# D added to the raw filter, its transposes evacuated in halves, and a new sequence, in a four-layer long-convolution and MLP kernel

## The chip, the cores and the metric

The kernel runs on one core of a Trainium2 chip. Its engines are TensorE (PE in the profile, PEld its weight loads), VectorE (DVE), ScalarE (ACT), GpSimd (POOL) and SyncE (SP), which here only issues DMAs. The metric is the device time of one execution in microseconds (us). The time before is the median of three runs, 240.48 us (239.6, 240.48 and 241.68).

## The reference

The input x is 2048 positions by 512 channels in bfloat16, and four layers are applied to it, each added to its input: A, B, A, B.

```python
def _A_ref(q, k, v, shift_k, ssm_k, ssm_D):
    for t in range(ks):                       # ks = 4
        k_shift = k_shift + k_pad[:, t:t + S, :] * shift_k[:, ks - 1 - t]
    kv = k_shift * v
    y = irfft(rfft(pad(kv)) * rfft(pad(ssm_k)))[:S]     # causal convolution, 2048 taps per channel
    y = y + kv * ssm_D
    return q * y

def _B_ref(x, w1, b1, w2, b2):                # 512 -> 1376 -> 512
    h = gelu(einsum(layernorm(x), w1) + b1)
    return einsum(h, w2) + b2

x = x + A(layernorm(x), k, v, ...);  x = x + B(layernorm(x), ...)
x = x + A(layernorm(x), k, v, ...);  x = x + B(layernorm(x), ...)
```

Only q of layer A depends on x; the convolution y depends on k, v and the filter alone, so it is the same for both A layers.

## The kernel before, in words

The kernel computes y once, in front, and then walks through the 16 groups of positions (a group is 128 positions, one per partition) twice: normalise, multiply by y and add (layer A), normalise and run the MLP (layer B).

**The convolution** is a length-4096 Fourier transform made of matmuls. The filter (ssm_k, 512 channels by 2048) arrives in four slabs b = 0..3 of 128 channels, 512 KB each, in the region R_HRAW. For each slab 16 transposes (tag "ht", line 523), each on every sixteenth column, turn it into two PSUM banks; one copy (BOTH, that is ACT or DVE, line 450) moves it to R_HP; an add (line 447) of D on one partition row then puts the skip term kv * D into the filter's tap 0. Stage 1 (h1, line 540) takes 16 matmuls per eight channel groups into a two-bank tile, 16 tiles in all, each emptied by one "evac" (line 450); stage 2 (h2, line 553) is 16 tiles of eight matmuls with weights from tab_s, 16 slabs of 256 KB. Sixteen DMAs from SBUF to SBUF then make a half-swapped copy of the filter's spectrum.

The shifted k times v is made in two ways: for channel blocks 0 and 1 by transposes (line 584), matmuls with tap diagonals (line 601) and a DVE multiply out of PSUM (line 608), for blocks 2 and 3 by eight DVE operations each on 128 x 2048 elements (line 447). Its stage 1 (x1, line 540 again) and stage 2 (x2, line 646) follow; after stage 2 come 16 DVE products with the filter's spectrum (line 447, called "the products"), which read four rotating buffers; then the inverse stages i1 (line 669) and i2 (line 726).

**The layers.** Per group of positions: bn_stats and bn_aggr on DVE (749, 751), a power on POOL (755, 757), a normalising tensor_scalar (763), the products with y (447); then z is transposed by PE (809) or by DMA (802), m1 (822) with its Gelu on ACT (827) and m2 (855) with its add on DVE (859).

**Warm-up.** Before the filter lands, PE multiplies a tile of zeros eight times (line 496); POOL clears the tile (line 490).

**The order of the work.** Every operation is recorded by P.op with the regions it reads and writes. A written-out table, ORDER, gives the sequence of all operations; each engine executes its own in that sequence, in order. SECOND names the operations that go to the second of their two allowed engines, and BANKS the first PSUM bank of every tile. Waits are derived from these: an operation that reuses a bank waits for the reader of the tile that had it last. SP also issues its DMAs in this order, so a DMA that waits holds back the ones behind it.

The change and the prediction touch the filter's transposes and the D add (516 to 530), the zero tile (489, 490), the table preload (462), the DMA queues, and the order of everything up to about 85 us. The region R_T2 of the inverse table (L444) overlies k.

Of the kernel before, what the change touches and what calls it, by code (L numbers as in the profile page):

```python
# [7 lines left out]
ALU = mybir.AluOpType  # L8
# [30 lines left out]
class Prog:  # L39
# [280 lines left out]
def _tables():  # L320
# [32 lines left out]
    T2 = np.stack([np.cos(ps), -np.sin(ps)], 2) / 2048  # L353
    T2 = T2.reshape(128, 4096)
    return F, S2, U, T2


AR = 105600
PE_CH, PO_CH = (0, 1), ()
LOADS = ("k", "v") + tuple(range(16))  # L360
PARTS = ((0, 64), (64, 64))
BLOCKS0, BLOCKS1 = (1,1,2,2,2,2,2,2,2), (4, 4, 4, 4)
NSPLIT = 4


def bass_interleave_layers__ssm_conv_h3__mixer_channel_mlp__prompt_kernel(
        nc, A_q, A_k, A_v, A_shift_k, A_ssm_k, A_ssm_D, B_x, B_w1, B_b1, B_w2, B_b2, out):
    P = Prog(nc)
# [54 lines left out]
    R_W = place(512)  # L423
# [29 lines left out]
    BOTH = (ACT, DVE)  # L453
# [442 lines left out]
```

## Time and profile before

| | us |
|---|---|
| median of three runs | 240.48 |
| the profiled execution | 239.94 |
| its span | 238.1 |
| PE busy | 226.6 |
| DVE busy | 177.2 |
| ACT busy | 141.8 |
| POOL busy | 32.5 |

The span runs from the first to the last instruction of the program; the profiled execution's own time has 1.84 us around it. A line such as "4.99 1.86 PE L523 ... x16" says: from 4.99 us on, for 1.86 us, sixteen instructions of line 523 on PE; in brackets stands how long the engine was idle before and what ended the wait. Lines of a helper (447 for element-wise operations, 450 for evictions, 436 and 444 for DMAs) gather many steps; the operand shapes tell them apart.

### The profile page before, as it was taken

Reading aid. Unit: us, or ns where it says so; the run is one execution under the profiler, and the core shown is the slowest. Engines: PE = TensorE matmul, PEld = TensorE weight load, DVE = VectorE, ACT = ScalarE, POOL = GpSimd, SP = SyncE. Lnnn points to the kernel's source line nnn. Section 1 sums busy time; section 2 is a strip of 40 time slices with the busy share of each in tenths; the row PEclk is TensorE's granted clock in tenths of the full one; section 3 lists DMA queues with packets and bytes.
Section 4 is the critical chain, followed back from the end, with each engine's and each line's share of the span. In section 5 each row is a group of like instructions: output and inputs, shape, how many; then the busy total and the mean of one; then the engine's idle time right before and its main releaser. Section 6 shows DMA issues by size and latency. Waiting matters only on the chain.

```text
span 238.1 us, 5549 instructions
## 1 busy us (share of the span) xinstructions
PE 226.6 (95%) x2312; PEld 152.1 (64%) x2332; DVE 177.2 (74%) x360; ACT 141.8 (60%) x225; POOL 32.5 (14%) x70
## 2 busy tenths in 40 slices
PE   7997999977999999999999999999999999999996
PEld 3886777866899886867577676554444444444544
DVE  0799999999999999999987799959271783311124
ACT  2599999999999983746246552474335245067000
POOL 1140000001013431332120130040022001000000
PEclk9999999999999999999999999999999999999999
DMA  6999947999990005120222022205104003301033
GB/s 222 367 347 383 384 120 201 293 283 270 379 310 2 3 3 67 21 51 0 44 44 47 0 48 44 45 1 69 22 0 88 3 0 65 111 0 47 6 110 105
DMA packets 37035, 27.40 MB, mean 115 GB/s; under 512 B 19506, under 2 KB 29969, under 8 KB 37010
## 3 DMA queue, kind: packets, MB, share of 16 engines
q1 hardware_dynamic: 36446, 26.91, 38.7%
q8 instruction: 18, 0.29, 0.5%
q10 hardware_dynamic: 564, 0.14, 0.4%
q14 instruction: 7, 0.06, 0.1%
HBM read 16.82 MB, written 2.10 MB: 79 GB/s over the span
## 4 chain that ended last, share of the span: by engine, by line
PE 81%; ACT 13%; DMA 2%; DVE 2%; issue 2%
PE ps L822 32%; PE ps L855 31%; ACT ar L450 12%; PE ps L669 5%; PE ps L540 4%; PE ps L726 3%; PE ps L601 2%; DMA ar<-in_A_ssm_k_dram 2%; PE ps L523 1%; PE ps L844 1%; DVE ar L450 1%; PE ps L646 1%; PE ps L553 1%; ACT L462 1%; DVE ar L608 1%
## 5 line engine op out<-in xcount | busy, mean ns | idle before, releaser
L827 ACT ACTIVATE ar<-ps,sm 128x256 bf16<-128x256 f32 (+4 forms) x143 | 66.1, 524 | 70.2 <-PE ps L822 66.4
L822 PE MATMUL ps<-ar 128*128 128x256 bf16 (+3 forms) x567 | 82.1, 296 | 0.2
L855 PE MATMUL ps<-ar 128*128 128x512 bf16 (+1 forms) x330 | 78.2, 379 | 0.7
L450 ACT ACTIVATE ar<-ps 128x1024 bf16<-128x1024 f32 (+2 forms) x80 | 73.2, 1065 | 5.3 <-PE ps L508 3.6
L822 PEld LDWEIGHTS ps<-ar 128*128 128x128 bf16 (+1 forms) x572 | 53.0, 100 | 28.9 <-ACT ar L827 1.2
L447 DVE TENSOR_TENSOR ar<-ar 128x512 bf16<-128x512 bf16 (+3 forms) x106 | 64.9, 640 | 1.0
L855 PEld LDWEIGHTS ps<-ar 128*128 128x128 bf16 (+1 forms) x341 | 33.2, 98 | 35.1
L859 DVE TENSOR_TENSOR ar<-ar,ps 128x512 bf16<-128x512 bf16 x31 | 20.8, 678 | 37.5 <-PE ps L855 37.5
L749 DVE BATCH_NORM_STATS2 sm<-ar 128x6 f32<-128x512 bf16 (+1 forms) x68 | 43.1, 649 | 0.6
L763 DVE TENSOR_SCALAR ar<-ar,sm 128x512 bf16<-128x512 bf16 x64 | 24.7, 403 | 8.3 <-POOL sm L757 6.7
L757 POOL TENSOR_TENSOR sm<-sm 128x2 f32<-128x2 f32 (+2 forms) x26 | 20.6, 790 | 2.2
L755 POOL TENSOR_SCALAR sm<-sm 128x2 f32<-128x2 f32 (+2 forms) x26 | 5.4, 209 | 111.5 <-DVE sm L751 111.1
L540 PE MATMUL ps<-ar 128*64 128x128 bf16 x512 | 16.8, 220 | 0.4 <-ACT ar L450 0.2
L540 PEld LDWEIGHTS ps<-ar 128*64 128x64 bf16 x512 | 14.8, 110 | 2.2 <-ACT ar L450 0.4
L669 PE MATMUL ps<-ar 128*128 128x128 bf16 x256 | 15.1, 220 | 0.9 <-ACT ar L450 0.9
L669 PEld LDWEIGHTS ps<-ar 128*128 128x128 bf16 x256 | 14.6, 114 | 1.3 <-ACT ar L450 0.8
L450 DVE CAST ar<-ps 128x1024 bf16<-128x1024 f32 (+1 forms) x13 | 14.9, 1175 | 0.0
L450 DVE COPY ar<-ps 128x2048 bf16<-128x2048 bf16 (+1 forms) x7 | 7.0, 995 | 7.2 <-PE ps L523 6.9
L646 PE MATMUL ps<-ar 128*128 128x64 bf16 x256 | 9.3, 193 | 2.6 <-ACT ar L450 2.6
L751 DVE BATCH_NORM_AGGREGATE sm<-sm 128x2 f32<-128x6 f32 (+1 forms) x64 | 10.6, 174 | 1.0
L646 PEld LDWEIGHTS ps<-ar 128*128 128x128 bf16 x256 | 8.1, 98 | 3.7 <-ACT ar L450 3.5
L553 PE MATMUL ps<-ar 128*128 128x128 bf16 x128 | 8.6, 219 | 0.2
(33 smaller groups left out, 73.7 us busy)
## 6 DMA issues: line engine op xcount, KB each, us to landing
ar<-tab_s SPq DMA_DIRECT2D x16, 256.0 KB, 10.1
ar<-ar SPq DMA_DIRECT2D x16, 256.0 KB, 4.8
ar<-in_A_ssm_k_dram SPq DMA_DIRECT2D x4, 512.0 KB, 5.9
ar<-in_A_k_dram SPq DMA_DIRECT2D x8, 256.0 KB, 7.5
ar<-in_A_v_dram SPq DMA_DIRECT2D x8, 256.0 KB, 10.1
ar<-in_A_q_dram SPq DMA_DIRECT2D x4, 512.0 KB, 7.1
out_dram<-ar SPq DMA_DIRECT2D x7, 256.0 KB, 2.0
ar<-in_B_w_dram SPq DMA_DIRECT2D x1, 1376.0 KB, 8.8
```

What stands on the lines that cost most here:

```text
L447: return P.op(eng, lambda e: e.tensor_tensor(o, a, b, op), reads=[a, b] + list(more), writes=[o])
L450: f = {ACT: lambda e: e.activation(dst, src(), AF.Copy), DVE: lambda e: e.tensor_copy(dst, src())}
L540: r = e.matmul(Q(tl, 64 * ri, 64, i * 128, [1, 128]), w, m, start=True, stop=True)
L646: r = e.matmul(Q(tl, 0, 128, i * pitch, [1, n]), w, m, start=True, stop=True)
L669: r = e.matmul(Q(tl, 0, 128, i * 128, [1, 128]), w, m, start=q == 0, stop=q == 1)
L749: P.op(DVE, lambda e, sj=sj, x=x: e.bn_stats(sj, x), reads=[x], writes=[sj])
L757: P.op(POOL, lambda e: e.tensor_tensor(r, v, hf, ALU.pow), reads=[v, hf], writes=[r])
L763: P.op(DVE, lambda e: e.tensor_scalar(o, x, m, r, ALU.subtract, ALU.mult), reads=[x, m, r], writes=[o])
L822: r = e.matmul(Q(tl, 0, rows, 0, [1, w]), a, m, start=dk == 0, stop=dk == 3)
L827: P.op(ACT, lambda e, dst=dst, tl=tl, rows=rows, bias=bias, w=w: e.activation(dst, Q(tl, 0, rows, 0, [1, w]), AF.Gelu_apprx_tanh, bias=bia ...
L855: r = e.matmul(Q(tl, 0, 128, 0, [1, 512]), ins[fc][0], ins[fc][1], start=fc == 0, stop=fc == 10)
L859: P.op(DVE, lambda e, x=x, tl=tl: e.tensor_tensor(x, x, Q(tl, 0, 128, 0, [1, 512]), ALU.add), reads=[x], writes=[x], tile=tl)
```

## The change

It does four things.

1. **D.** The four D adds on one partition row of R_HP are gone. In their place four matmuls with one column each turn D into a column per slab (tile "dcol"), and four DVE adds on 128 x 1 elements put them into column 0 of the raw slabs, ahead of the transposes that read that column.
2. **Halves.** Each slab's 16 transposes are two groups of eight (columns 15 to 8, then 7 to 0), each with one bank and its own copy. Only the second group reads the column with D.
3. **Zero tile.** It is 128 x 128 and may be cleared by DVE or POOL; the warm-up matmuls read it four times over as a 128 x 512 operand. The number and size of the warm-up matmuls is as before.
4. **ORDER, SECOND and BANKS** are new. The sequence is another one up to the first m1 tiles and the same behind them, but for the numbers.

```diff
+HSPLIT = (0, 1, 2, 3)
-    z = A(0, 128, R_W, [1, 512])
-    P.op(POOL, lambda e, z=z: e.memset(z, 0.0), writes=[z])
+    z = A(0, 128, R_W, [1, 128])
+    z4 = A(0, 128, R_W, [0, 4], [1, 128])
+    P.op((DVE, POOL), lambda e, z=z: e.memset(z, 0.0), writes=[z])
...
-            r = e.matmul(Q(tl, 0, 128, 0, [1, 512]), z[:, :128], z, start=True, stop=True)
+            r = e.matmul(Q(tl, 0, 128, 0, [128, 4], [1, 128]), z, z4, start=True, stop=True)
...
+    P.tag = "dcol"
+    dcol = Tile(1)
+    ins = [A(0, 1, R_D + 128 * b, [1, 128]) for b in range(4)]
+
+    def f(e, ins=ins):
+        for b in range(4):
+            r = e.matmul(Q(dcol, 0, 128, b, [1, 1]), ins[b], one[:, :1], start=True, stop=True)
+        return r
+    P.op(PE, f, reads=[one] + ins, tile=dcol).preds[warm.i] = "psum"
+    for b in range(4):
+        h = A(0, 128, R_HRAW + b * 2048, [1, 1])
+        P.op(DVE, lambda e, h=h, b=b: e.tensor_tensor(h, h, Q(dcol, 0, 128, b, [1, 1]), ALU.add),
+             reads=[h], writes=[h], tile=dcol)
...
     for b in range(4):
-        tl = Tile(2)
-        src = [A(0, 128, R_HRAW + b * 2048 + a, [16, 128]) for a in range(16)]
...
-        o = A(0, 1, R_HP + b * 2048, [64, 32], [1, 4])
-        tt(o, o, A(0, 1, R_D + 128 * b, [4, 32], [1, 4]), ALU.add, (DVE, POOL))
+        cuts = ((15, 14, 13, 12, 11, 10, 9, 8), (7, 6, 5, 4, 3, 2, 1, 0)) if b in HSPLIT else (tuple(range(15, -1, -1)),)
+        for cut in cuts:
+            tl = Tile(len(cut) // 8)
+            a0 = cut[-1]
+            src = [(a, A(0, 128, R_HRAW + b * 2048 + a, [16, 128])) for a in cut]
+
+            def f(e, src=src, tl=tl, a0=a0):
+                for a, x in src:
+                    r = e.transpose(QB(tl, 0, 128, (a - a0) * 128, [1, 128]), x, IDN)
+                return r
+            P.op(PE, f, reads=[x for _, x in src] + [IDN], tile=tl).preds[warm.i] = "psum"
+            evac(BOTH, A(0, 128, R_HP + b * 2048 + 4 * a0, [4, len(cut)], [64, 32], [1, 4]),
+                 lambda tl=tl, n=len(cut): QB(tl, 0, 128, 0, [128, n], [4, 32], [1, 4]), tl)
```

Line numbers move: in the changed kernel the warm-up is line 499, dcol 511, its adds 516, the taps 524 (508 before), the filter's transposes 542 (523 before), h1 and x1 557 (540), evictions 452 (450), element-wise operations 449 (447), DMAs 438 and 446 (436 and 444), i1 686 (669).

**The opening, PE and DVE.** PE before, from the warm-up to the end of h1:

```order
L496 MATMUL ps<-ar 128x512 x8
L523 MATMUL ps<-ar 128x128 x16
L508 MATMUL ps<-ar 128x512 x2
L523 MATMUL ps<-ar 128x128 x16
L540 MATMUL ps<-ar 64x128 x64
L523 MATMUL ps<-ar 128x128 x32
L540 MATMUL ps<-ar 64x128 x192
```

and PE now:

```order
L499 MATMUL ps<-ar 128x512 x8
L511 MATMUL ps<-ar 128x1 x4
L542 MATMUL ps<-ar 128x128 x8
L524 MATMUL ps<-ar 128x512 x2
L542 MATMUL ps<-ar 128x128 x24
L557 MATMUL ps<-ar 64x128 x48
L542 MATMUL ps<-ar 128x128 x8
L557 MATMUL ps<-ar 64x128 x32
L542 MATMUL ps<-ar 128x128 x24
L557 MATMUL ps<-ar 64x128 x176
```

The dcol matmuls stand ahead of all transposes, the first slab's second half comes behind the taps, and three of the last slabs' halves stand between two h1 groups. DVE, before, up to its first shift products (128x2048):

```order
L450 COPY ar<-ps 128x16x32x4
L447 TENSOR_TENSOR ar<-ar 1x32x4
L450 COPY ar<-ps 128x16x32x4
L447 TENSOR_TENSOR ar<-ar 128x512
L450 CAST ar<-ps 128x128x8
L450 COPY ar<-ps 128x16x32x4 x2
L450 CAST ar<-ps 128x128x8 x3
L447 TENSOR_TENSOR ar<-ar 128x2048 x5
```

and DVE now:

```order
L493 MEMSET ar 128x64
L516 TENSOR_TENSOR ar<-ar,ps 128x1
L452 COPY ar<-ps 128x8x32x4
L516 TENSOR_TENSOR ar<-ar,ps 128x1
L452 COPY ar<-ps 128x8x32x4 x2
L452 CAST ar<-ps 128x128x8
L516 TENSOR_TENSOR ar<-ar,ps 128x1 x2
L452 COPY ar<-ps 128x8x32x4 x4
L452 CAST ar<-ps 128x128x8 x3
L449 TENSOR_TENSOR ar<-ar 128x2048 x5
```

Seven of the eight half copies are on DVE, the tap diagonal (128x512) has gone to POOL, and the h1 evictions (128x128x8) on DVE are four as before. The 128x8x32x4 CAST that followed later on DVE (one h2 tile) is gone; that tile is on ACT now.

**ACT's start.** Before, from its DMA issues to the second stage of the filter (128x8x32x4):

```order
L444 DMA ar<-tab_small 128x384
L436 DMA ar<-in_A_shift_k_dram 1x2048
L436 DMA ar<-in_A_ssm_D_dram 1x512
L436 DMA ar<-in_A_shift_k_dram 128x2x4
L450 ACT_TABLE_LOAD
L450 ACTIVATE ar<-ps 128x512 x2
L450 ACTIVATE ar<-ps 128x128x8 x2
L462 ACT_TABLE_LOAD
L450 ACTIVATE ar<-ps 128x128x8 x10
L450 ACTIVATE ar<-ps 128x16x128
L450 ACTIVATE ar<-ps 128x8x32x4 x13
```

and now (line 464 is the preload, 462 before):

```order
L446 DMA ar<-tab_small 128x384
L438 DMA ar<-in_A_ssm_D_dram 1x512
L438 DMA ar<-in_A_shift_k_dram 1x2048
L464 ACT_TABLE_LOAD
L438 DMA ar<-in_A_shift_k_dram 128x2x4
L452 ACTIVATE ar<-ps 128x512 x2
L452 ACTIVATE ar<-ps 128x8x32x4
L452 ACTIVATE ar<-ps 128x128x8 x12
L452 ACTIVATE ar<-ps 128x16x128
L452 ACTIVATE ar<-ps 128x8x32x4 x15
```

One table load is left, ahead of all evictions; one half copy (the first 128x8x32x4) has come to ACT.

**SP, from the last loads of v to the half-swaps (64x8x256).** Before:

```order
L436 DMA ar<-in_A_v_dram 128x1024 x3
L444 DMA ar<-tab_s 128x1024 x4
L436 DMA ar<-in_B_b_dram 128x10x1
L436 DMA ar<-ar 64x8x256 x8
L444 DMA ar<-tab_small 128x1024
L436 DMA ar<-ar 64x8x256 x3
```

and now:

```order
L438 DMA ar<-in_A_v_dram 128x1024 x2
L446 DMA ar<-tab_s 128x1024
L446 DMA ar<-tab_small 128x1024
L446 DMA ar<-tab_s 128x1024
L438 DMA ar<-ar 64x8x256
L438 DMA ar<-in_B_b_dram 128x10x1
L438 DMA ar<-ar 64x8x256 x6
```

The first quarter of the inverse table (tab_small, 128x1024) stands ahead of the last slab of tab_s; it waits for DVE's last read of k in the shifts.

More of the change, by code (lines that the diff above doesn't have):

```diff
@@ L45 @@
     ORDER = (
[41 rows of a table removed]
[42 rows of a table added]
     SECOND = (
-        53, 56, 57, 59, 62, 63, 65, 66, 78, 84, 88, 98, 112, 162, 172, 174, 186, 188, 208, 240, 276, 317, 342, 385)
+        61, 63, 67, 69, 71, 73, 75, 81, 87, 89, 93, 171, 179, 181, 197, 209, 223, 249, 281, 316, 351, 394)
     BANKS = (
[7 rows of a table removed]
[7 rows of a table added]
     def __init__(self, nc):
@@ L487, in bass_interleave_layers__ssm_conv_h3__mixer_channel_mlp__prompt_kernel, with f @@
     tload(t_sm, row, 384, R_U, 256)
-    z = A(0, 128, R_W, [1, 512])
-    P.op(POOL, lambda e, z=z: e.memset(z, 0.0), writes=[z])
+    z = A(0, 128, R_W, [1, 128])
+    z4 = A(0, 128, R_W, [0, 4], [1, 128])
+    P.op((DVE, POOL), lambda e, z=z: e.memset(z, 0.0), writes=[z])
     P.tag = "warm"
     tl = Tile(2)
-    def f(e, tl=tl, z=z):
+    def f(e, tl=tl, z=z, z4=z4):
         for i in range(8):
-            r = e.matmul(Q(tl, 0, 128, 0, [1, 512]), z[:, :128], z, start=True, stop=True)
+            r = e.matmul(Q(tl, 0, 128, 0, [128, 4], [1, 128]), z, z4, start=True, stop=True)
         return r
@@ L500, in bass_interleave_layers__ssm_conv_h3__mixer_channel_mlp__prompt_kernel @@
     one = A(0, 1, R_ONE, [1, 128])
-    P.op(POOL, lambda e: e.memset(one, 1.0), writes=[one])
+    P.op((POOL, DVE), lambda e: e.memset(one, 1.0), writes=[one])
+    P.tag = "dcol"
[10 more added lines that the diff above has]
+             reads=[h], writes=[h], tile=dcol)
     P.tag = "taps"
@@ L517, in bass_interleave_layers__ssm_conv_h3__mixer_channel_mlp__prompt_kernel @@
     for b in range(4):
-        tl = Tile(2)
-        src = [A(0, 128, R_HRAW + b * 2048 + a, [16, 128]) for a in range(16)]
-        def f(e, src=src, tl=tl):
-            for a in range(16):
-                r = e.transpose(QB(tl, 0, 128, a * 128, [1, 128]), src[a], IDN)
-            return r
-        P.op(PE, f, reads=src + [IDN], tile=tl).preds[warm.i] = "psum"
-        evac(BOTH, A(0, 128, R_HP + b * 2048, [4, 16], [64, 32], [1, 4]),
-             lambda tl=tl: QB(tl, 0, 128, 0, [128, 16], [4, 32], [1, 4]), tl)
-        o = A(0, 1, R_HP + b * 2048, [64, 32], [1, 4])
-        tt(o, o, A(0, 1, R_D + 128 * b, [4, 32], [1, 4]), ALU.add, (DVE, POOL))
+        cuts = ((15, 14, 13, 12, 11, 10, 9, 8), (7, 6, 5, 4, 3, 2, 1, 0)) if b in HSPLIT else (tuple(range(15, -1, -1)),)
[10 more added lines that the diff above has]
+                 lambda tl=tl, n=len(cut): QB(tl, 0, 128, 0, [128, n], [4, 32], [1, 4]), tl)
     def stage1(src, G, gk, g0, dg0, n):
```

97 rows, old and new, of tables (BANKS, ORDER) are left out of this document.

## The prediction

> **What bounds the kernel now.** I read the page's first part, then a table of stretches, then the chain of work that ended last, and then the opening 26 us instruction by instruction.
>
> ```profile
> span 238.1 us, 5549 instructions
> ...
> PE 226.6 (95%) x2312; PEld 152.1 (64%) x2332; DVE 177.2 (74%) x360; ACT 141.8 (60%) x225; POOL 32.5 (14%) x70
> ```
> ```profile
> core 0: us, PE busy (x) PEld busy (x) DVE busy (x) ACT busy (x) POOL busy (x), PEclk, DMA share, GB/s
> ...
> 50.00:55.00 5.00, 3.22 (x96) 2.89 (x96) 5.00 (x6) 5.00 (x7) 0.00 (x0) 1.00 0.90 241
> 55.00:60.00 5.00, 3.82 (x94) 3.38 (x91) 5.00 (x5) 4.98 (x6) 0.63 (x1) 1.00 1.02 318
> ...
> 65.00:70.00 5.00, 5.00 (x92) 5.00 (x90) 5.00 (x7) 5.00 (x7) 0.00 (x0) 1.00 1.04 362
> ...
> 90.00:238.00 148.00, 145.06 (x833) 82.32 (x846) 95.34 (x243) 60.36 (x123) 19.09 (x36) 1.00 0.19 41
> ```
> The 95% of PE hides two programs. After 90 us PE works 145.06 of 148.00 us and nobody else is full. Between 50 and 60 us it is the other way round: DVE and ACT have no free moment, PE idles 2.96 us. The chain says where the one becomes the other:
>
> ```profile
> 0.73 4.21 DMA ar<-in_A_ssm_k_dram
> ...
> 16.80 14.72 ACT ar L450 x15
> ...
> 47.22 2.12 PE ps L646 x64
> ...
> 49.36 1.77 ACT ar L450 x2
> ...
> 62.30 1.05 ACT ar L450
> 63.35 0.05 issue
> 63.40 8.35 PE ps L669 x144
> ```
> From 63.40 on the chain is PE almost without a break. The order behind that point is the same but for some rows around 70 to 85 us, so **the end moves by what the start of this run moves**. What leads up to it is emptying of PSUM by ACT and DVE, and the products on DVE. I therefore price the change in ACT and DVE time before 63 us. Nothing in PE's tail is removed.
>
> **The opening before.**
>
> ```profile
> 0.73 0.52 POOL L490 MEMSET ar<- 128x512 bf16 x1 [0.29 <-POOLq L881]
> ...
> 1.31 3.60 PE L496 MATMUL ps<-ar 128*128 128x512 bf16 x8 [1.31 <-POOL ar L490]
> ...
> 4.99 1.86 PE L523 MATMUL ps<-ar 128*128 128x128 bf16 x16
> ...
> 6.79 0.60 PE L508 MATMUL ps<-ar 1*128 1x512 bf16 x2
> ...
> 6.89 1.24 DVE L450 COPY ar<-ps 128x2048 bf16<-128x2048 bf16 x1 [6.89 <-PE ps L523]
> ...
> 7.32 1.22 PE L523 MATMUL ps<-ar 128*128 128x128 bf16 x16
> 7.42 1.09 ACT L450 ACTIVATE ar<-ps 128x512 bf16<-128x512 f32 x2 [3.64 <-PE ps L508]
> ...
> 8.24 0.21 DVE L447 TENSOR_TENSOR ar<-ar 1x128 bf16<-1x128 bf16 x1
> ...
> 8.51 1.99 PE L540 MATMUL ps<-ar 128*64 128x128 bf16 x64
> ...
> 9.19 1.02 ACT L450 ACTIVATE ar<-ps 128x1024 bf16<-128x1024 f32 x1 [0.68 <-PE ps L540]
> ...
> 11.58 1.28 ACT L462 ACT_TABLE_LOAD   x1
> ...
> 12.88 7.69 ACT L450 ACTIVATE ar<-ps 128x1024 bf16<-128x1024 f32 x8
> ```
> ```profile
> 24.00 14.84 ACT L450 ACTIVATE ar<-ps 128x1024 bf16<-128x1024 f32 x16
> ```
> ```profile
> 17.49 5.75 DVE L447 TENSOR_TENSOR ar<-ar 128x2048 bf16<-128x2048 bf16 x5
> 23.26 1.23 DVE L450 COPY ar<-ps 128x2048 bf16<-128x2048 bf16 x1
> 24.40 1.21 DVE L450 CAST ar<-ps 128x1024 bf16<-128x1024 f32 x1
> 25.53 2.35 DVE L447 TENSOR_TENSOR ar<-ar 128x2048 bf16<-128x2048 bf16 x2
> ```
> ```profile
> L450 ACT ACTIVATE ar<-ps 128x2048 bf16<-128x2048 bf16 x1 | 1.9, 1933 | 0.0
> L450 DVE COPY ar<-ps 128x512 bf16<-128x512 bf16 x2 | 0.8, 406 | 0.0
> ```
> Neighbours overlap a little, so I price by pace: an ACT eviction costs (14.84 - 1.02)/15 = 0.92 us from start to start, a DVE one 25.53 - 24.40 = 1.13 us, a 16-transpose copy 1.14 us on DVE. A half tile (1024 bf16) lies between 406 and 1230 ns; linear in the size that is 0.68 us alone and, in a row, about 0.6 us. On ACT I take half of 1.93, so 0.95 us.
>
> **The change, part by part.**
>
> *Halves.* DVE's first copy waited for 16 transposes (4.99 to 6.85). The first copy now waits for 8: half of 1.86 saves 0.93 us, first copy at about 5.95. Taps follow these 8, so ACT starts about 0.45 us sooner, near 6.95. Seven halves on DVE cost 7 x 0.6 = 4.2 us against 4 x 1.14 = 4.56; one half goes to ACT, +0.95.
>
> *D into the raw rows.* One DVE add (0.21) and three POOL adds go; four 128x1 adds out of PSUM come on DVE. No such row exists; the bounds are 0 and the 0.21 of the 1x128 add, and I take 0.15, together 0.6 us. New on PE: four one-column matmuls behind the warm-up, and behind them, in PE's order, every transpose now waits for the D row. D's landing has no row. It is issued right behind the identity table, whose landing is
>
> ```profile
> ar<-tab_small ACTq DMA_DIRECT2D x1, 96.0 KB, 3.7
> ```
> that is 0.74 + 3.7 = 4.4 us, and before, the taps (issued just ahead of D) were in use at 6.79 without a wait. So D lands between 4.4 and 6.8; up to 4.9 it costs nothing because the filter lands at 4.95, at 6.8 it costs 1.8 us. I take 4.4, the nearest row: one small packet right behind that table.
>
> *Zero tile.* DVE clears 128x128 in place of POOL's 128x512 (0.52 us, which ends the wait of 1.31 ahead of the warm-up). I take 0.4 us earlier warm-up. It buys no work: the first transposes still wait for the filter at 4.95. The bounds are nothing and 0.4 us.
>
> *ACT's tables.* Before, a table is loaded in the idle opening and a second one at 11.58, between evictions. In the new order the Gelu table is loaded first and Copy follows with no other load: -1.30 us (11.58 to 12.88), in the busy stretch. [...]
>
> *New sequence, up to the channel transposes' eviction.* I walk the new rows by hand: PE takes 0.5 us for a group of 8 transposes or an h1 tile of 16 matmuls (1.99 us for four, 1.22 us for 16 transposes with their tail), and its result can be read 0.2 us later (8.51 + 0.5 to 9.19). PE's first groups can be read at 5.95, 6.95 (taps), 7.4, 7.9 and 8.4, the first h1 tiles at 8.9 and 9.4.
> On DVE this gives: copies 5.95 to 6.6, 7.4 to 8.0, 8.4 to 9.0; an h1 eviction 9.4 to 10.55; two adds and a copy to 11.45; three copies, which arrive from 11.9 on, to 13.7; then PE has h1 tiles again at 14.4, and three evictions end at 17.8. The work is 9.3 us (4.2 + 0.6 + 4 x 1.13), the waits 2.6. The first shift product begins at 17.8 against 17.49. But one eviction (1.13) of the filter's second stage has left DVE behind that point. **DVE: 0.8 us sooner at the end of the shifts**; with no wait at all 3.4.
> On ACT: taps at 6.95, the half at 7.9, 12 h1 evictions from 8.9. Twelve times 0.92 is 11.0; it waits 0.3 us among the first and 0.5 us where three transpose groups stand ahead of the next h1 tile. So the 1.93 us eviction begins at 20.7; before it began some 1.8 us ahead of the eviction at 24.00, at 22.2. That is 1.5 us sooner (the 1.30 of the table among it). One eviction more follows on ACT (16 of the second stage, not 15), which takes 0.92 back. **ACT: 0.6 us sooner**; with no wait 1.4.
>
> *Middle.* The products start when DVE has finished its shifts and the first two channel blocks are evicted. Before, ACT waited once there:
>
> ```profile
> 42.75 40.83 ACT L450 ACTIVATE ar<-ps 128x1024 bf16<-128x1024 f32 x45 [0.23 <-PE ps L540]
> ```
> By the new order two of its evictions, the third x1 one and the first of channel block 1, come behind DVE's shifts, about 0.3 us of wait each; I take 0.3 from ACT's gain. So DVE's sixteen products
>
> ```profile
> 49.16 18.32 DVE L447 TENSOR_TENSOR ar<-ar 128x2048 bf16<-128x2048 bf16 x16
> ```
> begin near 48.4, and ACT is 0.3 us ahead in the sixteen that lead up to PE's run:
>
> ```profile
> 48.29 15.05 ACT L450 ACTIVATE ar<-ps 128x1024 bf16<-128x1024 f32 x16
> ```
> Both engines are full here and feed each other through four buffers, so the end lies between ACT's 0.3 and DVE's 0.8: I take **0.6 us**. What is late next is PE itself: i1's second half needs the last product, 67.5 before, and PE came to it five tiles into its run, at 63.40 + 5 x 8.35/9 = 68.0, so 0.5 us of cover.
>
> *SP.* The load of the inverse table (256 KB, L446) overwrites k and waits for DVE's last read of it; it now stands ahead of the last slab of stage-two weights and of the first half-swaps, so these wait too. Issue and landing bound it:
>
> ```profile
> 17.25 2.35 SPq L444 DMA_DIRECT2D ar<-tab_s  x4
> ```
> ```profile
> ar<-ar SPq DMA_DIRECT2D x1, 256.0 KB, 2.7
> ```
> ```profile
> ar<-tab_small SPq DMA_DIRECT2D x1, 256.0 KB, 4.6
> ```
> From that read the slab needs 0.1 + 0.6 + 2.7 = 3.4 us on an idle queue, 5.3 on a full one. PE comes to its use three DVE operations (3.4 us) and one PE tile (0.5) later, 3.9 to 4.0. I take 2.7, since all earlier loads have landed by then; the cost is nothing, the other end +1.3.
>
> *70 to 85 us.* Statistics and m1 tiles are reordered with the same instructions. PE waits there neither before nor, by the order of its inputs, after: its z transposes still come behind the bulk of the i2 matmuls. I take nothing.
>
> **Sum.** 239.94 us is the profiled run: span 238.1 and 1.84 around it. 239.94 - 0.6 = 239.3. That run lies 0.54 below the median of the three, 240.48; on the median's footing the forecast is **239.9 us**.
>
> **Rivals.**
>
> *The clock comes late* (slower than before). The rows above show PE at half pace in the opening: 16 transposes take 1.86 us at 4.99, 1.22 at 7.32; the pace turns between the two, 5.5 to 6 us after the warm-up began at 1.31. The new order has gaps of its own right there, between the warm-up's end near 4.4 and the slab's landing, and behind the first half. If the next four groups and h1 tiles, until about 10 us, still go at 0.93 us instead of 0.5, that is 4 x 0.43 = 1.7 us, for which DVE and ACT wait. Net 1.7 - 0.6 = +1.1: **241.6**. It decides if the second slab's 8 transposes still take 0.9 us. For it: the gaps. Against: they are 0.5 us. [...]
>
> *The weight slab is late.* The 4.6 us landing instead of 2.7: 1.3 us at that tile, with all of the x1 groups behind it in PE's order: 239.9 + 1.3 = **241.2**.
>
> *The waits vanish.* If my walk puts too much idle time into both engines, DVE gains up to 3.4 us and ACT 1.4, and if the middle then hands some of DVE's work time back to ACT, the end lies half-way: 2.4 us, **238.1**.
>
> *Nothing arrives.* ACT and DVE are both full from 50 to 63 us; if the products wait for ACT's channel evictions, the head start ends there: **240.5**.
>
> **Chances.** Forecast 0.58 (own range 239.1 to 240.7), late clock 0.12, late slab 0.10, waits vanish 0.13, nothing 0.07. The range for 8 in 10 is 238.0 to 241.9: it takes in the ends of ACT's idle time, D's landing at its middle, and the rivals in part. One per cent is 2.4 us, about what a measurement tells from no change. Faster by that, below 238.1: most of the vanished waits and a little of the forecast, 0.11; slower, above 242.9: D at 6.8, or clock and slab together, 0.09; within: 0.80.
>
> **What would show it.** First DVE copy near 6.0; one table load, ahead of the first eviction; the 2048-wide ACT eviction near 20.7; first shift product at 17.8; first of sixteen products near 48.4; PE's long run of i1 matmuls (L686, L669 before) from about 62.8. Wrong if PE's long run begins where it did, if the transposes wait for D, or if the tail behind 85 us takes another time than before.

## The result, and the profile after

The changed kernel takes 242.22 us (median of nine runs, 241.51 to 243.53) where the kernel before takes 240.48 us (nine runs, 239.6 to 241.68): a ratio of 1.0078, 95% interval 1.0050 to 1.0106 (the ratios here are not formed from the medians, and differ from theirs by up to 0.003). The forecast was 239.9 us, with a range of 238.0 to 241.9: the change makes the kernel 1.7 us slower where a gain of 0.6 us was forecast.

The profiled execution took 241.57 us. Its page begins:

```profile
span 239.8 us, 5558 instructions
...
PE 226.3 (94%) x2317; PEld 152.1 (63%) x2336; DVE 175.2 (73%) x365; ACT 142.2 (59%) x226; POOL 32.9 (14%) x67
```

DVE has 2.0 us less to do than before (177.2), ACT 0.4 us more; the span is 1.7 us longer. So it is waiting that grew. The chain of work that ended last (start, length, what) shows where:

```profile
14.94 1.01 issue
...
20.53 1.73 issue
22.62 10.13 ACT ar L452 x10
...
63.66 1.05 ACT ar L452
64.76 11.98 PE ps L686 x208
```

PE's long i1 run begins at 64.76; before, it began at 63.40, and the prediction said 62.8. Behind that point 175.0 us remain, before 174.7. So the loss lies ahead of the run, as the prediction said the gain would. The two longest of the chain's pieces called "issue" in front of it make 2.74 us, where the kernel before has none over 0.46: time in which the engine waited for nothing that the profile shows. PE's own rows:

```profile
11.16 1.71 PE L542 MATMUL ps<-ar 128*128 128x128 bf16 x24
12.80 2.13 PE L557 MATMUL ps<-ar 128*64 128x128 bf16 x63
15.95 3.75 PE L557 MATMUL ps<-ar 128*64 128x128 bf16 x113 [1.01 <-issue]
19.63 0.90 PE L601 MATMUL ps<-ar 128*128 128x128 bf16 x13
22.26 0.33 PE L601 MATMUL ps<-ar 128*128 128x128 bf16 x3 [1.73 <-issue]
```

The second stop is the telling one. L601 is a group of 16 transposes of k (the first that feed the shift on PE). The program puts its waits ahead of a group; inside one there is nothing to wait for. PE did 13 transposes, stood still for 1.73 us, and did the other three. The kernel before has a stop at nearly the same time, but between two groups:

```profile
14.04 5.38 PE L540 MATMUL ps<-ar 128*64 128x128 bf16 x160 [0.17 <-ACT ar L450]
20.12 1.05 PE L584 MATMUL ps<-ar 128*128 128x128 bf16 x16 [0.69 <-ACT ar L450]
22.16 1.07 PE L584 MATMUL ps<-ar 128*128 128x128 bf16 x16 [0.98 <-issue]
```

What this did to the engines that PE feeds, ACT first and then DVE:

```profile
13.48 1.94 ACT L452 ACTIVATE ar<-ps 128x1024 bf16<-128x1024 f32 x2 [0.72 <-PE ps L557]
16.20 5.61 ACT L452 ACTIVATE ar<-ps 128x1024 bf16<-128x1024 f32 x6 [0.78 <-PE ps L557]
22.62 11.96 ACT L452 ACTIVATE ar<-ps 128x2048 bf16<-128x2048 bf16 x12 [0.82 <-PE ps L601]
```

Before, ACT came to the same 2048-wide eviction (the second of this row's two instructions, at 22.24) without a wait:

```profile
21.33 2.84 ACT L450 ACTIVATE ar<-ps 128x1024 bf16<-128x1024 f32 x2
```

DVE, after:

```profile
16.65 2.35 DVE L452 CAST ar<-ps 128x1024 bf16<-128x1024 f32 x2 [0.89 <-PE ps L557]
18.92 5.88 DVE L449 TENSOR_TENSOR ar<-ar 128x2048 bf16<-128x2048 bf16 x5
...
30.33 1.22 DVE L625 TENSOR_TENSOR ar<-ps,ar 128x1024 bf16<-128x1024 f32 x1 [0.99 <-issue]
...
50.39 18.40 DVE L449 TENSOR_TENSOR ar<-ar 128x2048 bf16<-128x2048 bf16 x16
```

ACT is out of work at 21.80 and waits 0.82 us for the three missing transposes. DVE begins its shifts at 18.92 (before 17.49), saves one eviction (1.13) and waits 0.99 us at 30.33, for shift matmuls (L618, at 28.45) that themselves waited 0.45 us for a bank which ACT emptied late: 1.43 - 1.13 + 0.99 = 1.29, and its products begin 1.23 us later than before (50.39 against 49.16).

**What PE waits for.** The trace also records DMA packets. A queue of its own, of kind "instruction", carries packets of 16,384 bytes:

```profile
q1 hardware_dynamic: 36446, 26.91, 38.6%
q8 instruction: 18, 0.29, 0.5%
```

(columns: packets, MB, share of the 16 DMA engines). That this queue is PE's is taken from the match that follows. I counted PE's matmuls and weight loads in order of time. Both stops of the changed kernel come behind the 443rd and the 694th, 251 apart, and PE goes on 2.3 to 2.4 us after the start of such a packet (2.3 to 2.6 in the other kernels below that stop). Counted with the semaphore waits and the one drain that the trace also records on PE, the stops in the table below come behind PE's 449th and 705th instruction in every kernel, 256 apart; 251 is such a block less its waits. All times in us; "entered" is when PE did the first instruction of the block before, taken as 251 matmuls and weight loads earlier:

```
kernel             entered  packet  PE on   | entered  packet  PE on   PE stood
before              10.00   13.32   15.73   |  15.73   19.77   22.16   behind the group of 16
changed              9.62   13.61   15.95   |  15.95   19.89   22.26   inside it, 13 done
changed, again      11.63   14.37   16.97   |  16.97   20.78   23.28   inside it, 13 done
32 warm-ups         10.38   14.07   16.54   |  16.54   20.44   23.01   in the h1 tiles
four loads at once  13.15   14.04   no stop |  18.27   19.94   no stop
parts alone          9.28   13.18   no stop |  15.37   19.52   21.90   inside it, 14 done
table alone          9.78   13.12   15.63   |  15.63   19.56   22.06   behind it
one matmul for D     9.71   13.63   16.01   |  16.01   19.89   22.39   behind it
the same, padded     9.60   13.47   15.85   |  15.85   19.77   22.16   inside it, 13 done
```

So the author's theory, called FETCH below: PE gets its instructions in blocks, the next block is asked for when PE enters a block, and between 5 and 30 us, where the DMA engines' busy share is 1.00 to 1.08, the request stands some 4 us behind the bulk loads (3.7 to 4.1 us in most rows of the table). The request itself has no record in the trace. From entering a block to having the next one takes some 6.3 us (22.26 - 15.95; 5.3 to 6.5 in the other rows without the limit on loads).

### The profile page after: what moved, and what is told of

The parts are those of the page before. It is cut to its first block, busy times and chain, and to the rows that moved or that the text cites. A ratio compares the mean times of both kernels' runs of the same rounds, so it can differ in the third digit from the quotient of the medians.

```text
span 239.8 us, 5558 instructions
## 1 busy us (share of the span) xinstructions
PE 226.3 (94%) x2317; PEld 152.1 (63%) x2336; DVE 175.2 (73%) x365; ACT 142.2 (59%) x226; POOL 32.9 (14%) x67
## 3 DMA queue, kind: packets, MB, share of 16 engines
q1 hardware_dynamic: 36446, 26.91, 38.6%
## 4 chain that ended last, share of the span: by engine, by line
PE 78%; ACT 14%; issue 3%; DMA 2%; DVE 1%; ACTq 0%; DVEq 0%
PE ps L839 31%; PE ps L872 31%; ACT ar L452 14%; PE ps L686 5%; PE ps L743 3%; PE ps L557 2%; DMA ar<-in_A_shift_k_dram 2%; PE ps L542 2%; PE ps L618 1%; PE ps L861 1%; DVE ar L452 1%; PE ps L570 1%; PE ps L601 0%; ACT ar L844 0%; ACTq L438 0%
## 5 line engine op out<-in xcount | busy, mean ns | idle before, releaser
L839 PE MATMUL ps<-ar 128*128 128x256 bf16 (+4 forms) x567 | 82.1, 296 | 0.6 <-issue 0.4
L452 ACT ACTIVATE ar<-ps 128x1024 bf16<-128x1024 f32 (+2 forms) x82 | 75.3, 1063 | 7.0 <-PE ps L524 3.2
L449 DVE TENSOR_TENSOR ar<-ar 128x512 bf16<-128x512 bf16 (+2 forms) x104 | 64.1, 643 | 0.9
L774 POOL TENSOR_TENSOR sm<-sm 128x2 f32<-128x2 f32 (+2 forms) x26 | 20.7, 796 | 2.2
L452 DVE CAST ar<-ps 128x1024 bf16<-128x1024 f32 (+1 forms) x12 | 13.8, 1175 | 2.2 <-PE ps L557 2.0
L686 PEld LDWEIGHTS ps<-ar 128*128 128x128 bf16 x256 | 14.5, 114 | 1.4 <-DVE ar L449 1.0
L768 DVE BATCH_NORM_AGGREGATE sm<-sm 128x2 f32<-128x6 f32 x64 | 10.5, 174 | 0.9
L663 PEld LDWEIGHTS ps<-ar 128*128 128x128 bf16 x256 | 8.3, 98 | 3.6 <-ACT ar L452 3.5
L570 PEld LDWEIGHTS ps<-ar 128*128 128x128 bf16 x128 | 7.4, 97 | 1.8 <-issue 1.7
```

The costliest lines, as they stand in the source:

```text
L449: return P.op(eng, lambda e: e.tensor_tensor(o, a, b, op), reads=[a, b] + list(more), writes=[o])
L452: f = {ACT: lambda e: e.activation(dst, src(), AF.Copy), DVE: lambda e: e.tensor_copy(dst, src())}
L570: r = e.matmul(Q(tl, 0, 128, i * n, [1, n]), w, m, start=True, stop=True)
L686: r = e.matmul(Q(tl, 0, 128, i * 128, [1, 128]), w, m, start=q == 0, stop=q == 1)
L774: P.op(POOL, lambda e: e.tensor_tensor(r, v, hf, ALU.pow), reads=[v, hf], writes=[r])
L839: r = e.matmul(Q(tl, 0, rows, 0, [1, w]), a, m, start=dk == 0, stop=dk == 3)
```

## The experiments

Besides FETCH two rivals are tested: SEQUENCE (PE stops because the new order makes its groups wait for evictions or banks) and BALANCE (the sixteenth second-stage eviction on ACT is the whole loss). All kernels are timed beside the kernel before, whose median was 240.39, 240.16 and 240.20 us in the three groups of four.

**32 warm-ups: do the stops follow the instruction count or the work?**

```diff
-        for i in range(8):
-            r = e.matmul(Q(tl, 0, 128, 0, [128, 4], [1, 128]), z, z4, start=True, stop=True)
+        for i in range(32):
+            r = e.matmul(Q(tl, 0, 128, 0, [1, 128]), z, z, start=True, stop=True)
```

> The changed kernel, with the warm-up written as 32 matmuls of 128 columns in place of 8 of 512: the same PE time, but 24 more matmuls and 24 more weight loads at PE's head. Theory FETCH: PE's instructions come in blocks of some 251 matmuls and weight loads (a 16 KB packet each on a queue of its own), and in the saturated stretch a block cannot arrive sooner than 6.3 us after PE entered the block before; PE stops in the middle of a group where a block ends, after 443 and after 694 matmuls and weight loads in the changed kernel (14.72 to 15.95 and 20.31 to 22.26). It expects the two stops after 443 and 694 again, that is 48 instructions earlier in the work: the first within the h1 tiles at about 14.0, the second still among the h1 matmuls and not in the shift transposes (L601), PE going on at about 15.2 and 21.5; the time within 0.7 us of 242.2. Rival SEQUENCE: PE stops because the new order makes these tiles wait for evictions or banks. It expects the stops at the same matmuls as before the edit (the tile at 15.95 and the first transposes of L601).

Measured: 243.26 us, ratio 1.0115 (1.0066 to 1.0163). PE's rows:

```profile
16.54 4.43 PE L557 MATMUL ps<-ar 128*64 128x128 bf16 x128 [0.63 <-issue]
23.01 0.44 PE L557 MATMUL ps<-ar 128*64 128x128 bf16 x9 [2.04 <-issue]
23.49 1.87 PE L601 MATMUL ps<-ar 128*128 128x128 bf16 x16
```

The stops follow the count: behind 443 and 699 matmuls and weight loads (694 expected; with the waits counted it is 705 as before), the second now in the h1 tiles, and L601 runs through its 16 transposes. SEQUENCE falls as the account of the stops. PE was slow in the opening of this execution (the 24 transposes of L542 took 2.78 us, 1.71 in the changed kernel) and goes on 1.3 to 1.5 us later than expected; the time is 0.4 us above the band.

**Four loads at once: is it the queue of bulk loads that holds the fetch up?**

```diff
+    sp = [P.ops[i] for i in P.ORDER if P.ops[i].dma and P.ops[i].engs == (SP,)][:41]
+    for x, y in zip(sp[4:], sp[8:]):
+        y.preds[x.i] = "raw"
     P.arrange()
```

> The changed kernel, with each of SP's loads from the ninth to the last table slab waiting until the load four before it on SP has landed, so that at most four (about 1 MB) are under way; nothing else differs. FETCH expects the instruction packets to start sooner after PE enters a block (1 to 2.7 us in place of 3.9), PE's stops near 15 and 21 us to shrink by 1 us or more each, the 2048-wide ACT eviction at 21.2 to 21.9 in place of 22.62, the long i1 run of PE at 63.0 to 64.0 in place of 64.76, and 240.5 to 241.5 in place of 242.2. SEQUENCE and BALANCE (the sixteenth second-stage eviction on ACT is the whole loss) expect the stops and the time unchanged, or later where a slab now lands later (up to +1).

Measured: 245.86 us, ratio 1.0233 (1.0184 to 1.0282). For the first two blocks the mechanism came as expected: the packets start 0.9 and 1.7 us after PE enters a block, not 2.7 to 4.2 as in the other rows of the table, and PE has no stop at a block's end. The time went the other way, since four loads do not fill the DMA engines (busy share 0.71 to 0.94 between 8 and 24 us, 1.00 to 1.08 in the changed kernel) and the tables and v come late:

```profile
33.42 1.26 PE L570 MATMUL ps<-ar 128*128 128x128 bf16 x16 [0.65 <-DMA ar<-tab_s]
```
```profile
40.98 1.23 DVE L625 TENSOR_TENSOR ar<-ps,ar 128x1024 bf16<-128x1024 f32 x1 [3.20 <-DMA ar<-in_A_v_dram]
```

So at the two stops the wait from entry to packet goes with the loads in flight (3.99 and 3.94 us with all of them, 0.9 and 1.7 with four), but this is no remedy. The third block of this run does not fit: its packet starts at 27.31, 4.3 us after PE entered the block at 22.99, though the loads are still limited; this stays unexplained. The changed kernel shows a short latency without any edit: between 30 and 35 us its DMA engines are a third busy, and the packet of 32.97 starts 0.6 us after PE entered its block at 32.37. At this place it is under 1.5 us in the other profiles too, except for 1.9 us with 32 warm-ups and 2.8 us in the run with the sixteenth eviction below, which FETCH does not explain.

```profile
20.00:25.00 5.00, 3.00 (x52) 2.73 (x50) 4.97 (x6) 4.18 (x4) 0.00 (x0) 1.00 1.04 381
25.00:30.00 5.00, 3.94 (x51) 3.15 (x50) 4.34 (x4) 5.00 (x7) 0.00 (x0) 1.00 1.05 384
30.00:35.00 5.00, 4.66 (x63) 3.89 (x63) 4.67 (x5) 5.00 (x6) 0.00 (x0) 1.00 0.33 120
```

(stretch, length, busy time of PE, PEld, DVE, ACT, POOL, granted clock, DMA share, GB/s)

**Parts alone: D, the halves and the zero tile in the old order.** The tables keep before's order, engines and banks, with each group of 16 transposes, its eviction and its add replaced by the new pieces; D's column is copied once so that its bank comes free:

```diff
     P.op(PE, f, reads=[one] + ins, tile=dcol).preds[warm.i] = "psum"
+    dc = M(0, 128, M_DEP + 12, [1, 4])
+    P.op(DVE, lambda e: e.tensor_copy(dc, Q(dcol, 0, 128, 0, [1, 4])), writes=[dc], tile=dcol)
```

> D in the raw rows, the halves and the smaller zero tile, with the order, the engines and the banks of the kernel before for everything else (the second table load on ACT among it); the D column is copied out of PSUM once so that its bank comes free. SEQUENCE expects the loss gone: the halves' head start arrives, 239.5 to 240.3. FETCH expects that the eight more instructions of dcol put the end of a block inside the first group of shift transposes (before, it lay right behind that group), PE stands there until about 22.2, ACT's 2048-wide eviction starts at 22.4 to 22.7 (22.24 before), and nothing of the head start is left: 240.3 to 241.2.

Measured: 240.80 us, ratio 1.0012 (0.9974 to 1.0050), what FETCH expected. PE stops inside the group, and goes on at 21.90:

```profile
20.02 0.94 PE L603 MATMUL ps<-ar 128*128 128x128 bf16 x14 [0.66 <-ACT ar L452]
21.90 1.18 PE L603 MATMUL ps<-ar 128*128 128x128 bf16 x18 [0.94 <-issue]
```

It costs little here: ACT reaches its 2048-wide eviction at 22.22 (before 22.24; 22.4 to 22.7 was expected), since in this order it is busy that long (no gap from 13.85 on). The head start of the halves is not seen either: PE waited 0.41 and 0.35 us for D's adds on DVE in this order, and DVE's first shift product is at 17.70 against 17.49.

**The new order alone, twice.** The kernel before with the new order, banks and engines. In the first of the two runs the assignment of D's adds and of the zero tile made PE wait for POOL in the opening; in the second that is mended in part.

> The opposite: the kernel before (whole slabs of 16 transposes, D added to the turned filter, 128x512 zero tile) in the new order, with the new banks and engines, the table loaded once. SEQUENCE expects most of the loss: 241.5 to 242.5. FETCH expects PE to stop again at the ends of blocks (about 443 and 694 instructions, going on at 15.7 to 16.1 and 22.1 to 22.4), with the first shift transposes just complete ahead of the second stop, since dcol's eight instructions are missing: ACT's 2048-wide eviction near 21.5, and 240.5 to 241.7.

Measured: 244.15 us, ratio 1.0153 (1.0118 to 1.0188). PE waited 1.85 us for POOL at 10.86, and everything behind it moved; this says nothing on the question.

> The new order, banks and engines on the kernel before, as in the earlier run, but with two faults of that run mended: POOL clears the warm-up's tile first, the first slab's D add is on DVE, and POOL makes its tap diagonal behind the D adds, so that no transform waits for them. FETCH expects PE's second stop behind the first shift transposes (no dcol, eight instructions fewer), DVE's three last h1 evictions of the first stage still behind PE's first stop, first shift product 18.6 to 19.2, long i1 run 63.5 to 64.0, and 240.4 to 241.1. SEQUENCE expects the loss to stay, 241.8 to 242.3.

Measured: 241.14 us, ratio 1.0033 (1.0015 to 1.0051), just above what FETCH expected and 0.7 us under SEQUENCE. The second stop lies behind the group (PE on at 22.87, packet at 20.41), DVE's shifts begin at 19.57, later than expected: PE still waited three times for POOL, 1.4 us in all. (The long i1 run began at 65.22 in its profile, where PE's granted clock was 0.62 between 60 and 64 us, so that number is no measure.) So without the parts the new order is 0.9 us slower than the kernel before (240.20), less than the whole change; how much of that is the order and how much the waits for POOL was not separated.

**One matmul for D: six instructions fewer.**

```diff
-    dma(A(0, 1, R_D, [1, 512]), dr(A_ssm_D, 0, [0, 1], [1, 512]), eng=ACT)
+    dma(A(0, 4, R_D, [1, 128]), dr(A_ssm_D, 0, [128, 4], [1, 128]), eng=ACT)
...
-        for b in range(4):
-            r = e.matmul(Q(dcol, 0, 128, b, [1, 1]), ins[b], one[:, :1], start=True, stop=True)
-        return r
+        return e.matmul(Q(dcol, 0, 128, 0, [1, 4]), d4, i4, start=True, stop=True)
```

(d4 is D on four partitions, i4 the corner of the identity.)

> The changed kernel with D loaded on four partitions and turned into its column by one matmul in place of four: three matmuls and three weight loads fewer at PE's head, nothing else. In the changed kernel PE stopped at 20.31 with 13 of the 16 first shift transposes done, five or six instructions short of the group's end. FETCH (blocks of instructions) expects the stop to lie behind that group now: PE still stands from about 20.5 to 22.2, but ACT's 2048-wide eviction no longer waits for it and begins right behind the h1 evictions at 21.8 to 21.9 in place of 22.62; 0.3 to 0.8 us of that reach the end: 241.4 to 241.9. SEQUENCE and BALANCE expect no difference: 242.2.

Measured: 240.86 us, ratio 1.0041 (1.0015 to 1.0067): FETCH's sign and place, with more of it reaching the end than it had said. The ten runs spread from 240.06 to 242.52, and the profiled one is the shortest. PE, ACT and DVE:

```profile
19.61 1.07 PE L599 MATMUL ps<-ar 128*128 128x128 bf16 x16
22.39 1.07 PE L568 MATMUL ps<-ar 128*128 128x128 bf16 x16 [1.71 <-ACT ar L452]
```
```profile
17.07 19.29 ACT L452 ACTIVATE ar<-ps 128x1024 bf16<-128x1024 f32 x20 [0.83 <-PE ps L555]
```
```profile
18.90 5.88 DVE L449 TENSOR_TENSOR ar<-ar 128x2048 bf16<-128x2048 bf16 x5
...
29.36 1.22 DVE L623 TENSOR_TENSOR ar<-ps,ar 128x1024 bf16<-128x1024 f32 x1
...
49.43 18.26 DVE L449 TENSOR_TENSOR ar<-ar 128x2048 bf16<-128x2048 bf16 x16
```

The group is complete, ACT goes without a gap from 17.07 to 36.4 (its 2048-wide eviction at 21.61), DVE's wait of 0.99 us is gone, and PE's long run starts at 63.73 in place of 64.76. PE stands as long as before, at another place. The row gives ACT as what ended the stop; but ACT's last h1 eviction ends at 21.76, 0.6 us earlier, while 2.5 us behind the packet's start agrees with the other rows of the table.

**The same, padded: the six instructions back without D's old form.**

```diff
-    def f(e):
+    def f(e, z=z):
+        for i in range(3):
+            e.matmul(Q(dcol, 0, 128, 8, [1, 1]), z, z[:, :1], start=True, stop=True)
         return e.matmul(Q(dcol, 0, 128, 0, [1, 4]), d4, i4, start=True, stop=True)
```

> The kernel with D's column from one matmul, and ahead of that matmul three one-column matmuls whose result nobody reads: the six instructions are back, D's new form stays. FETCH expects the stop inside the first shift transposes again (13 of 16 done, on at 22.2 to 22.6), ACT's 2048-wide eviction 0.6 to 0.9 us after ACT came free, DVE waiting some 1 us for the first product of the fir group (L625), the long i1 run at 64.5 to 65, and 241.6 to 242.2. A rival by which D's load on four partitions or the single matmul made the gain expects 240.9 as without the three.

Measured: 242.07 us (four runs, 241.01 to 242.75), ratio 1.0084 (1.0051 to 1.0117). Three matmuls that nobody needs, 0.23 us of PE time in its idle opening, cost about 1 us at the end: 242.07 - 240.86 = 1.2 between the medians, 1.0 between the means (241.98 and 241.02), 0.9 between the starts of the long run (64.60 and 63.73). The two kernels were timed in different groups and their runs overlap, so the size is not sharp:

```profile
19.53 0.90 PE L601 MATMUL ps<-ar 128*128 128x128 bf16 x13
22.16 0.33 PE L601 MATMUL ps<-ar 128*128 128x128 bf16 x3 [1.73 <-issue]
```

ACT's 2048-wide eviction is at 22.52, DVE waits 0.99 us for L625, the long run starts at 64.60: the changed kernel's rows again. So this pair shows what the second stop does: six instructions move it in and out of the group, and ACT's and DVE's waits come and go with it.

**The table alone.** The kernel before, with operation 4, the Gelu table's load, moved in ORDER from between operations 78 and 82 to behind operation 2, the last of ACT's loads.

```diff
-        0, 47, 48, 6, 58, 59, 1, 49, 50, 7, 61, 3, 60, 79, 2, 62,
+        0, 47, 48, 6, 58, 59, 1, 49, 50, 7, 61, 3, 60, 79, 2, 4, 62,
```

> The kernel before with one edit, the Gelu table's load moved from between the evictions to behind ACT's DMA issues, so that only one table is loaded, in the idle opening. The prediction's term was -1.30 us on ACT. FETCH expects that most of it holds here, since the first shift transposes of this kernel are just complete when PE's block ends: ACT's 2048-wide eviction at 21.0 to 21.4 in place of 22.24, then some 0.3 us of wait, because PE goes on at 22.2 only; DVE is unchanged; the long i1 run at 62.7 to 63.3, 239.6 to 240.3. A rival by which ACT before 63 us does not set the end expects 240.4.

Measured: 240.19 us, ratio 1.0002 (0.9986 to 1.0018). The saving of 1.30 us buys nothing that can be measured, and here FETCH's numbers on ACT were wrong: its 2048-wide eviction is at 22.13, not at 21.0 to 21.4. ACT waits for h1 tiles in place of loading a table:

```profile
10.32 1.94 ACT L450 ACTIVATE ar<-ps 128x1024 bf16<-128x1024 f32 x2 [0.32 <-PE ps L540]
13.26 2.86 ACT L450 ACTIVATE ar<-ps 128x1024 bf16<-128x1024 f32 x3 [1.00 <-PE ps L540]
16.69 25.72 ACT L450 ACTIVATE ar<-ps 128x1024 bf16<-128x1024 f32 x27 [0.57 <-PE ps L540]
```

The three waits add to 1.89 us. The time lies in FETCH's band too (239.6 to 240.3), but no gain is seen, and the reason is neither FETCH's nor the rival's: ACT did not come forward at all.

**The sixteenth eviction.**

```diff
-        61, 63, 67, 69, 71, 73, 75, 81, 87, 89, 93, 171,
+        61, 63, 67, 69, 71, 73, 75, 81, 87, 89, 93, 123, 171,
```

(SECOND lists the operations on the second of their two engines; 123 is one eviction of the filter's second stage.)

> The changed kernel with one second-stage eviction, the one behind DVE's copy of the second channel's transposes, moved from ACT to DVE, where the kernel before had one at that place. BALANCE (the sixteenth eviction on ACT is the loss) expects ACT 0.92 us earlier from there on, the long i1 run at 63.8 and 241.3. FETCH counts that eviction as part of the loss only: DVE, which began its shifts 1.43 us later than in the kernel before, pays 1.13 us for it and regains the 0.99 us for which it waited at 30.33; so the products start at 50.2 to 50.5 as before the edit, and the time is 241.6 to 242.3.

Measured: 242.07 us, ratio 1.0084 (1.0055 to 1.0114). BALANCE, which said 241.3, falls: beside the changed kernel of the same group (241.80) the move gains nothing. The profile decides little here. It is of a long execution (242.72 us): the first stop lasted to 16.44, the second group of k's transposes took 1.73 us at 24.74 (1.06 in the changed kernel), the mean granted clock was 0.993, and the products begin at 52.26, where FETCH had 50.2 to 50.5.

**The changed kernel again.**

> The changed kernel once more, unchanged, for a second profile. FETCH expects PE's stops after 443 and after 694 matmuls and weight loads again, the second inside the first shift transposes, with PE going on 2.3 to 2.5 us after the instruction packet starts, and 242.2. A rival by which the profiled execution was an unlikely one expects no such stops, or others.

Measured: 241.80 us, ratio 1.0066 (1.0043 to 1.0088), with the same second stop; the first is not seen, since PE came to the end of that block later (16.97). The profiled execution was a long one, 243.09 us, and shows one source of the spread: PE's granted clock was 0.61 for 4 us of the opening, which it was not in the first profile.

```profile
8.00:12.00 4.00, 4.00 (x66) 3.73 (x65) 2.00 (x3) 2.52 (x4) 2.55 (x4) 0.61 0.98 300
```

**Exchange of two evictions, without and with the moved one.** On the kernel with one matmul for D: 87 is h1 tile 5, 101 is tile 12.

```diff
-        61, 63, 67, 69, 71, 73, 75, 81, 87, 89, 93, 171,
+        61, 63, 67, 69, 71, 73, 75, 81, 89, 93, 101, 171,
```

> The kernel with D's column from one matmul, and two first-stage evictions exchanged between the engines: DVE takes h1 tile 12, which is ready ahead of PE's first stop, and ACT tile 5 behind it. Theory CHAIN: the end goes with DVE's unbroken work from its first shift product to the products, and that work can begin sooner only if ACT frees the banks for the first shift matmuls (L616) in time. CHAIN expects the first shift product at 17.7 in place of 18.9, but ACT 0.8 later at its 2048-wide eviction (22.6), the shift matmuls done near 30 in place of 29.2, DVE waiting 1.5 to 2 us for them, and 241.2 to 241.7. A rival by which DVE's start alone sets the end expects 1.2 us less than without the exchange: 239.7.

Measured: 242.01 us, ratio 1.0075 (1.0044 to 1.0105). DVE's rows:

```profile
18.38 5.88 DVE L449 TENSOR_TENSOR ar<-ar 128x2048 bf16<-128x2048 bf16 x5
25.64 1.23 DVE L452 COPY ar<-ps 128x2048 bf16<-128x2048 bf16 x1 [1.38 <-PE ps L599]
...
30.89 1.23 DVE L623 TENSOR_TENSOR ar<-ps,ar 128x1024 bf16<-128x1024 f32 x1 [0.62 <-issue]
```

DVE starts sooner and then waits 2.0 us for PE, as CHAIN said, though most of it at another place, for the second group of k's transposes (L599). It starts 0.5 us sooner and not 1.2, because PE's first stop lasted to 16.62 here; the time is 0.3 us above the expected band. DVE's start alone does not set the end.

> The same exchange, and one second-stage eviction moved from ACT to DVE behind DVE's copy of the second channel's transposes. CHAIN expects DVE's wait for the first shift matmuls nearly gone (0 to 0.5 us), products from 49.2 to 49.8, and 240.3 to 241.0, no better than the kernel before, since what DVE gains at its start it pays in evictions. The rival (DVE's start alone) expects 239.9 to 240.8 as well, so the first of the two runs decides between them.

Measured: 241.88 us, ratio 1.0097 (1.0061 to 1.0132), worse than CHAIN had it by a microsecond. DVE's wait for the shift matmuls is gone, but the wait of 1.38 us for the second group of k's transposes, which CHAIN had left out, stays: ACT, one h1 tile more behind the first stop, frees PE's bank later (PE waits 0.48 us for it until 20.47, and stands another 1.80 us until 23.32). No version here beats the kernel before.

## Why the prediction was wrong, step by step

*Halves: right.* First copy at 5.75 (5.95 said), ACT's start at 6.50 (6.95 said: it counted half of the 0.93 us for the taps without a reason, and all of it came); three half copies in a row take 1.89 us, 0.6 each.

*D into the raw rows: right in what was counted.* PE waited for D until 4.51, ahead of the filter's landing; the adds take 0.15 to 0.16 us. Not counted: eight instructions more at PE's head. In the order before these cost nothing measurable (parts alone, ratio 1.0012); in the new one six instructions decide about 1 us.

*Zero tile: right.* The warm-up starts at 0.98, 0.33 us sooner, and nothing follows from it.

*ACT's tables: the load went as said (one, at 2.06), the -1.30 did not arrive.* In the kernel before, the table alone is worth 0.0 us (240.19 against 240.16): PE could not hand ACT its tiles sooner.

*New sequence: the step that failed.* The walk gave PE 0.5 us for every group as soon as its inputs were there. PE's instructions were not, and their supply, which the sum put at nothing, cost stops of 1.01 and 1.73 us: 18.92 for DVE's first shift product where the walk had 17.8, about the length of the first stop; 22.62 for ACT's 2048-wide eviction where it had 20.7, with 0.82 us of wait for three transposes and 0.72 and 0.78 before it, where the walk had 0.8 in all. "DVE 0.8 sooner" became 0.3 later (1.43 at the start, less the eviction of 1.13), and with the wait at 30.33, 1.29 later; ACT's 1.5 sooner at that eviction became 0.4 later, so that with the sixteenth eviction (0.92) its "0.6 sooner" became 1.3 later.

*Middle: not put to the test.* The prediction took a value between ACT's gain and DVE's; both became losses of about the same size. The products began at 50.39, not 48.4, and PE's run at 64.76, not 62.8.

*SP: right.* The inverse table's first quarter stands ahead of the last slab, and that slab lands 3.0 us after its issue at 36.49 (2.7 said), but PE comes to it at 40.11, with no wait:

```profile
36.49 0.43 SPq L446 DMA_DIRECT2D ar<-tab_s  x1
...
40.11 0.45 PEld L570 LDWEIGHTS ps<-ar 128*128 128x128 bf16 x8
40.12 0.62 PE L570 MATMUL ps<-ar 128*128 128x128 bf16 x8
```

*70 to 85 us and the tail: right within 0.3 us* (175.0 against 174.7 behind the run's start; 174.6 in the profile with one matmul for D).

*Rivals.* The late clock has the nearest number (241.6), but did not happen in the first profile: 24 transposes from 6.40 on take 1.71 us, less than 0.6 for eight, where its sign was 0.9. What slows the first transposes is not shown: in the kernel before, the granted clock is 1.00 from 4 to 8 us, where 16 of them take 1.86 us and the next 16 take 1.22. A low granted clock in the opening is seen in the second profile (0.61 from 8 to 12 us), and belongs to the spread of single runs. The late slab did not happen. "Nothing arrives" is nearest in kind: the head start was lost, but to blocks of instructions and not to full engines, and a stop was added.

Of the 1.7 us, about 1 is the stop inside the group, by the pair that differs in six instructions. What is left without it (240.86 against 240.16; 0.3 us in the profiles, 63.73 against 63.40) is put down to DVE's last h1 tiles, which the new order puts behind the first stop; this is argued from the rows, and no run separates it from the order's other effects.

The row that would have warned stood in the trace of before: 0.98 us ahead of L584 at 22.16, with "issue" as its cause. The prediction passed over it.

## What to carry to other kernels

An idle time that the profile puts down to "issue", in the middle of a group or at nearly the same time in two kernels, is worth asking what the engine's instructions wait for: look for the instruction packets and count the instructions between stops. Here, with the DMA engines' busy share at 1.00 to 1.08, PE got 251 matmuls and weight loads per 6.3 us, and work moved ahead of its stops arrived no sooner (first shift product at 18.92, before 17.49). Ask then whether a stop can fall behind a group that a free engine waits for, and not inside it: six instructions at the head decided that here, for about 1 us (240.86 against 242.07). Where that engine was busy anyway, as ACT in the old order, the place cost little (parts alone, ratio 1.0012).

## What the runs showed of the hardware

The changed kernel's trace has 18 packets of 16,384 bytes on the instruction queue, 0.5% of the time of the 16 DMA engines, where the queue of the loads has 38.6%. In the first two blocks behind 9 us, with a busy share of 0.98 to 1.08 (before, the changed kernel twice, one matmul for D), a packet starts 2.7 to 4.2 us after PE enters a block, mostly 3.7 to 4.1; with four loads in flight 0.9 and 1.7 us (but 4.3 in the third block); in the changed kernel at a share of 0.33, 0.6 us. In the table a PE that stands goes on 2.3 to 2.6 us after the packet's start. That the request is made when PE enters a block is inferred from these numbers, not recorded. Three one-column matmuls in an idle stretch (0.23 us at 4.74), some 16 us ahead of the stop that they move (20.43), changed the time by about 1 us (242.07 against 240.86).
